# Loading and preparing the first two row groups of a second feed-forward stage together, ahead of its first matmul

## The chip, the cores and the metric

The kernel runs on one core of one Trainium2 chip. The metric is device time in microseconds (us) of one execution; the kernel before has a median of 1038.68 us over 3 runs (1036.22 to 1038.87). In the rows that follow PE is TensorE, DVE is VectorE, ACT is ScalarE, POOL is GpSimd and SP is the engine that issues most DMAs.

## What is computed

Attention of 4 batches, 12 heads, 448 positions and 64 dimensions (causal), then a feed-forward layer in which each of the 1792 tokens goes through one of 8 experts, then a dense feed-forward layer:

```
logits = x @ w_gate;  e_idx = argmax(logits)
out[mask] = gate_w * eom * (relu(x[mask] @ w1[e]) @ w2[e])     # x: 1792 x 768, w1: 768 x 1024
h = x @ w_in                                                    # w_in: 768 x 2048
g = h - tanh(h)
y = g @ w_out                                                   # w_out: 2048 x 768
```

## The kernel before

Products are made of three matmuls of two half-precision parts (hi x hi, lo x hi, hi x lo). A weight or a row is therefore kept as two planes, hi and lo.

**Experts.** `slot` (L816 on) takes one block of 128 tokens through one expert: gathered rows, first product in two halves of four column blocks (`slot_mm1`), each followed by `slot_relu` (hi part `hh` on ScalarE L169, lo part `hl` on VectorE L170), transposes of the next block's rows (`rows_T`), the second product in two halves (`slot_mm2`, 8 blocks of three matmuls of 384 columns), each copied to `yo` by ScalarE (L832), and a store of the rows to `ys_d` in DRAM (L859). The rows of `ys_d` are sorted by expert. Expert e has a static slot and then extra slots under nested conditions (`extra`), as many as its token count asks for; the last expert (e = 7) has one extra slot in this run. Work that belongs to other parts is put between these pieces by `fill(z)`: z = 1 after the second `slot_relu`, 2 and 3 after the two output halves, 4 after the store. The argument `late` turns this on.

**w_in and w_out.** They come as pairs of 32-bit words of a double. `conv` turns 1024 of these into planes: `to_f32` (six VectorE operations on halves, L897, L900, L903), a scaling (`scaled`, ScalarE L113) and the lo part (`rest_of`, VectorE or GpSimd). `conv_load` brings a unit into one of two buffers `cu`, `conv_store` writes its planes (`co`) to `wb_d` in DRAM. The extra slots of expert 6 convert three units each, the static slot of expert 7 the last two that go through DRAM, and two more (`stg`) are converted after the last slot, in place. `wi_load(c)` brings chunk c of w_in (four chunks, 3072 elements in each of `wif[0]` and `wif[1]`, which lie in the experts' raw weight buffers `raw1` and `raw2`) back from `wb_d`; `wo_load(c)` does so for w_out.

**The last stage.** Its 14 row blocks go in groups of 3, 3, 3, 3 and 2. A block is prepared by `prep0` (load from `ys_d`, on SP's queue), `prep1` (maximum of each row and factors from it, VectorE), `prep_hi` (ScalarE), `prep_lo` (VectorE, or GpSimd for group 0), `prep_sc` (exponents, and two 128 x 128 diagonals per block), `prep2` (12 transposes on TensorE and two evictions into `yh` and `yl`) and `prep3` (product of ones with the diagonals, evicted into `rs`). `first_prep` does the first four steps for group 0, in the static slot of expert 7 (`fill(3)`). Group 1's rows are loaded after that slot. Its `prep1` to `prep_sc` run inside steps 0 to 7 of group 0, its `prep2` in steps 9 to 11 and its `prep3` in steps 12 and 13.

The loop over n (16 steps for each group, L1289 on) makes one column block of h per step (`a_mm`, 18 matmuls) and runs the tanh and its correction over four engines (`act_a` to `act_d`, the first operation being VectorE's L1229). From n = 17 on the blocks of w_out's product for the group before (`mm2_step`, L1272) are put between. PE, ACT, DVE and POOL each work strictly in the order in which the program lists their instructions, and SP issues its DMAs in its order too, waiting at each for what it needs.

Of the kernel before, what the change touches and what calls it, by code (L numbers as in the profile page):

```python
# [46 lines left out]
NDY = 22  # L47
# [10 lines left out]
def build(ctx: ExitStack, tc: tile.TileContext, kq0, kq, v, wg, wo, w1, w2, wf, out):  # L58
# [757 lines left out]
    def slot(e, i, w, tag, fill=None, trans=(), then=(), late=False):  # L816
# [21 lines left out]
        lo(0)  # L838
        slot_relu(1, slot_mm1(e, i, 1, w, tag), hh, hl)
# [68 lines left out]

    def conv(src, hi, lo, eng="v"):
        hs = [slice(0, 512), slice(512, 1024)]  # L910
        to_f32([(cc[:, h], src[:, h, :]) for h in hs])
        for h in hs:
            scaled("a", hi[:, h], cc[:, h].bitcast(F32))
        for h in hs:
            rest_of(eng, lo[:, h], cc[:, h].bitcast(F32), hi[:, h])
# [7 lines left out]
    def conv_fill(e, i):  # L923
        c = CPE[e] if e + 1 < E else 0
        n0 = c * (i - 1 - FB[e])
        p = (i - 1) % 2 if c == 3 else 0

        def fill(z):
            for j in range(c):
                if z == ((1,), (1, 3), (1, 2, 3))[c - 1][j]:  # L930
                    b = (p + j) % 2
                    conv(cu[b], co[b][:, 0], co[b][:, 1], "p" if j == 2 else "v")
                    conv_load(cu[b], unit_of(e, n0 + j + min(c, 2)))
                    conv_store(b, unit_of(e, n0 + j))

        return fill
# [28 lines left out]
    yg_of = lambda g, i: first["yg"][i] if g < 2 else yg1  # L965
# [49 lines left out]
    def prep_sc(g, i, n=1):  # L1015
# [5 lines left out]
                                       op0=ALU.mult, op1=ALU.mult)  # L1021
        for j in range(n):
# [4 lines left out]

    def prep2(g, i, tag="t"):
        d = G[g % 2]
        tsl = slice(i * 128, (i + 1) * 128)  # L1030
        planes_T(yq_of(g, i), d["yh"][:, :, tsl], d["yl"][:, :, tsl], tpool[0], tag, "v" if g == 1 else "a")
# [26 lines left out]
    def first_again():  # L1058
        for g in range(2):
            for i in range(GB[g]):  # L1060
                prep0(g, i, (GS[g] + i) * 128)
            if g == 0:
                first_prep()

# [20 lines left out]
    for e in range(E):  # L1085
# [25 lines left out]
        else:  # L1111
# [3 lines left out]
            stg += [wof[1][:, z * 2048 : (z + 1) * 2048] for z in range(2)]  # L1115
            tot = nc.values_load(flg[0:1, 1:2], min_val=0, max_val=NDY)
            remaining()
            first["yg"] = [wof[1][:, z * 2 * DM : (z + 1) * 2 * DM].bitcast(F32) for z in range(3)]
            at_ = (wof[1][:, 6 * DM :], wof[0])
            first["yq"] = [[t[:, z * 2 * DM : (z + 1) * 2 * DM].rearrange("p (k x n) -> p k x n", k=KD, x=2)  # L1120
                            for z in range(3)] for t in at_]
            first["dg"] = [[t[:, 6 * DM + 256 * z : 6 * DM + 256 * (z + 1)].bitcast(BF16).rearrange(
                "p (a n) -> p a n", a=2) for z in range(3)] for t in at_]
            first["sc"] = [t[:, 6 * DM + 768 : 6 * DM + 832].bitcast(F32) for t in at_]
            second = nc.values_load(flg[0:1, 0:1], engines=(SP,), min_val=0, max_val=128)
# [52 lines left out]
    qc = (cc, wof[0][:, 8192:10240].bitcast(U32))  # L1178
# [203 lines left out]
```

## Time and profile before

| | |
|---|---|
| median of 3 runs | 1038.68 us |
| the profiled execution | 1039.69 us |
| its span | 1038.0 us |
| TensorE busy | 985.1 us (95%) |
| VectorE busy | 787.2 us (76%) |
| ScalarE busy | 597.1 us (58%) |
| GpSimd busy | 470.4 us (45%) |
| mean granted TensorE clock | 0.992 |

Times in rows count from the start of the span. A row of the timeline gives start, duration, engine, line, operation, output and inputs, shape and count; what stands in brackets is the idle time of the engine before it and what ended that. A granted clock of 1.00 is full speed. A matmul's duration overlaps that of the next.

### The profile page before, as it was taken

What the parts mean: (1) busy time and instruction counts of PE and PEld (TensorE: products, weight loads), DVE (VectorE), ACT (ScalarE), POOL (GpSimd) and SP (SyncE); (2) the same over time, 40 slices, a digit from 0 to 9 for tenths busy, and PEclk for the clock granted to TensorE, in tenths of its full rate; (3) what the DMA queues carried; (4) which work ended last, traced back from release to release, by engine and by line L of the source; (5) the groups of instructions that cost most, each with busy time, mean ns of one, the idle gap of its engine ahead of it and who ended that gap; (6) DMA issues with size and microseconds to landing.
All of it is one profiled execution on the core that took longest, in us unless ns stands there. A gap on an engine that the chain in (4) does not pass through costs nothing. (4 is left out here: it accounts for less than half of the span.)

```text
span 1038.0 us, 24100 instructions
## 1 busy us (share of the span) xinstructions
PE 985.1 (95%) x9177; PEld 743.5 (72%) x9177; DVE 787.2 (76%) x1609; ACT 597.1 (58%) x1194; POOL 470.4 (45%) x499
## 2 busy tenths in 40 slices
PE   5999999998998999999988889999999999999996
PEld 4999999997777878777866555666666666667763
DVE  6668777786796678778778899887888798776640
ACT  5776777765456266563323679555656566555530
POOL 5475866584211021202228789545544443443321
PEclk9999999999999999999999999999999999999998
DMA  8889998955898879977887514010000000000000
GB/s 250 224 214 255 270 244 229 265 167 144 284 356 318 342 274 332 349 287 248 314 294 277 212 63 158 24 47 16 24 31 32 9 31 9 16 16 17 16 24 23
DMA packets 62646, 173.92 MB, mean 168 GB/s; under 512 B 8368, under 2 KB 23344, under 8 KB 59424
## 3 DMA queue, kind: packets, MB, share of 16 engines
q1 hardware_dynamic: 56352, 147.20, 42.4%
q0 software_dynamic: 6144, 24.84, 8.4%
q8 instruction: 79, 1.29, 0.5%
q14 instruction: 71, 0.58, 0.2%
HBM read 132.30 MB, written 29.62 MB: 156 GB/s over the span
## 5 line engine op out<-in xcount | busy, mean ns | idle before, releaser
L1272 PE MATMUL fo<-wo,g 128*128 128x384 f16 x1344 | 228.2, 326 | 0.0
L1221 PEld LDWEIGHTS <-raw 128*128 128x128 f16 x1440 | 140.7, 98 | 88.5 <-issue 10.1
L1272 PEld LDWEIGHTS <-g 128*128 128x128 f16 x1344 | 131.2, 98 | 83.8
L1231 POOL TENSOR_TENSOR V<-cu,cc 128x384 f32<-128x384 f32 (+1 forms) x80 | 78.7, 984 | 189.3 <-ACT cu L1230 188.5
L162 PEld LDWEIGHTS <-w 128*128 128x128 f16 x2592 | 148.7, 99 | 16.5 <-issue 15.5
L1221 PE MATMUL fh<-cu,raw 128*128 128x384 f16 (+1 forms) x864 | 131.9, 308 | 6.3 <-DVE cc L1229 6.3
L344 ACT ACTIVATE P<-s,nb 112x112 f32<-112x112 f32 (+1 forms) x192 | 89.8, 494 | 54.2 <-DVE nb L338 24.0
L381 PE MATMUL o<-v,PT 112*112 112x65 f32 x960 | 114.6, 259 | 0.0
L381 PEld LDWEIGHTS o<-v,PT 112*112 112x112 f32 x960 | 105.4, 178 | 0.1
L121 DVE SCALAR_TENSOR_TENSOR w<-raw,w 128x768 f16<-128x768 f32 (+1 forms) x99 | 99.0, 1062 | 3.6 <-ACT w L113 3.6
L800 POOL DMA_INDIRECT xg<-xs_d,idx x22 | 27.5, 1250 | 159.9 <-PEq L872 28.6
L1230 ACT ACTIVATE cu<-cc 128x384 f32<-128x384 f32 (+1 forms) x80 | 40.1, 502 | 103.4 <-DVE cc L1229 103.4
L1234 POOL TENSOR_TENSOR X<-cc,X 128x384 f32<-128x384 f32 (+1 forms) x80 | 91.2, 1140 | 4.1 <-ACT X L1233 0.5
L113 ACT ACTIVATE w<-raw 128x768 f16<-128x768 f32 (+2 forms) x106 | 89.1, 904 | 6.3 <-DVE w L121 3.7
L1229 DVE TENSOR_TENSOR cc<-fh,co 128x384 f32<-128x384 f32 (+1 forms) x80 | 42.0, 525 | 66.5 <-PE fh L1221 50.7
L331 DVE TENSOR_REDUCE s<-s 112x2 f32<-112x224 f32 (+1 forms) x144 | 78.9, 548 | 15.0 <-PE s L327 13.8
L1241 DVE SCALAR_TENSOR_TENSOR V<-cu,V 128x384 f32<-128x384 f32 (+1 forms) x80 | 85.2, 1065 | 0.1
L1249 DVE TENSOR_TENSOR V<-V,co 128x384 f32<-128x384 f32 (+1 forms) x64 | 78.3, 1224 | 0.0
L1221 PE MATMUL fh<-yh,raw 128*128 128x384 f16 x384 | 67.6, 326 | 0.7 <-DVE cc L1229 0.7
L362 PE MATMUL t<-ident,P 112*112 112x112 f32 x480 | 66.9, 262 | 0.0
L1250 ACT ACTIVATE g<-V 128x384 f16<-128x384 f32 (+1 forms) x80 | 40.1, 501 | 45.9 <-DVE V L1249 45.8
L325 PE MATMUL s<-kh,qa 128*112 128x112 f16 (+1 forms) x192 | 54.9, 294 | 10.1 <-POOL qa L276 7.0
(657 smaller groups left out, 2038.9 us busy)
## 6 DMA issues: line engine op xcount, KB each, us to landing
raw<-w SPq DMA_DIRECT2D x48, 512.0 KB, 6.8
raw<-w SPq DMA_DIRECT2D x60, 384.0 KB, 9.1
cu<-wf SPq DMA_DIRECT2D x22, 1024.0 KB, 7.1
wb_d<-co SPq DMA_DIRECT2D x22, 512.0 KB, 5.1
raw<-kq SPq DMA_DIRECT2D x11, 896.0 KB, 10.1
raw<-wb_d SPq DMA_DIRECT2D x8, 768.0 KB, 6.5
xs_d<-xq SPq DMA_DIRECT2D x24, 224.0 KB, 5.9
raw<-v SPq DMA_DIRECT2D x11, 448.0 KB, 10.7
```

Of the source, the lines that this page charges most:

```text
L113: nc.scalar.activation(out=out, in_=in_, func=AF.Copy, scale=WS)
L121: nc.vector.scalar_tensor_tensor(out=out, in0=in_, scalar=WS, in1=hi, op0=ALU.mult, op1=ALU.subtract)
L162: nc.tensor.matmul(out=ph[:, (f % 4) * 128 : (f % 4 + 1) * 128], lhsT=w[0][:, ww, k, f * 128 : (f + 1) * 128], rhs=xTs[tag][:, xx, k, :], ...
L331: nc.vector.tensor_reduce(out=d["nm", m], in_=d["s", m], op=ALU.max, axis=AX.X, negate=True)
L344: nc.scalar.activation(out=d["P"][:, j, OFF[i] : OFF[i] + n], in_=d["s", m][:, z, :], func=AF.Exp, bias=d["nb"][:, 2 * i + j : 2 * i + j + ...
L381: nc.tensor.matmul(out=po[:, i, :], lhsT=d["PT"][:, g, o : o + CP], rhs=d["t"][3][:, hl, j, :], start=(j == 0), stop=(j == i))
L1221: nc.tensor.matmul(out=ph[:, 0:nt], lhsT=wi[ww][:, f // 4, k, f % 4 * 128 : (f % 4 + 1) * 128], rhs=yy[:, k, 0:nt], start=(q == 0), stop=( ...
L1231: nc.gpsimd.tensor_tensor(out=d["V"], in0=d["U"], in1=d["h"], op=ALU.mult)
L1234: nc.gpsimd.tensor_tensor(out=d["X"], in0=d["h"], in1=d["X"], op=ALU.subtract)
L1241: nc.vector.scalar_tensor_tensor(out=d["V"], in0=d[f"S{z}"], scalar=QD[z - 1], in1=d["V"], op0=ALU.add, op1=ALU.mult)
L1249: nc.vector.tensor_tensor(out=d["V"], in0=d["V"], in1=rs_y(g, nt), op=ALU.mult)
L1272: nc.tensor.matmul(out=po[:, 0:384], lhsT=t[:, x, k, i * 128 : (i + 1) * 128], rhs=wo_[ww][:, k, z * 384 : (z + 1) * 384], start=(k == 0 a ...
```

## The change

Group 0's and group 1's rows now lie in w_in's chunks 2 and 3 (`rows_`), their planes in w_out's second buffer and in chunk 2 of `wif[1]`. All six loads go out at the start of the last expert. In its static slot a conversion is put between the two halves of the first product (new `fill(0)`, with a second buffer for the converted words), `first_prep` moves from `fill(3)` to `fill(2)`, and group 1's `prep1` goes into `fill(3)`. Chunks 0 and 1 of w_in are loaded after that slot, chunk 3 at step 0 and chunk 2 at step 4. After the last slot come group 0's diagonals on ScalarE (`prep_dg`), group 1's hi planes, the two staged conversions (scaled by ScalarE, VectorE before), group 1's exponents and lo planes, and only then group 0's transposes; then the lo parts of the staged units and group 1's diagonals. Group 1's transposes are in steps 2 to 4 (hi plane evicted by ScalarE, VectorE before) and its `prep3` in steps 5 and 6. In the extra slots of expert 6 the third unit's load and store move behind the store of the rows.

```diff
@@ slot
         hi(1)
         lo(0)
+        fill(0)
         slot_relu(1, slot_mm1(e, i, 1, w, tag), hh, hl)
@@ conv_fill
-                if z == ((1,), (1, 3), (1, 2, 3))[c - 1][j]:
-                    b = (p + j) % 2
+                at = ((1,), (1, 3), (1, 2, 3))[c - 1][j]
+                b = (p + j) % 2
+                if z == at:
                     conv(cu[b], co[b][:, 0], co[b][:, 1], "p" if j == 2 else "v")
+                if z == (4 if at == 3 else at):
                     conv_load(cu[b], unit_of(e, n0 + j + min(c, 2)))
                     conv_store(b, unit_of(e, n0 + j))
@@ prep_sc
+        if n > 1:
+            nc.vector.tensor_scalar(out=c(7), in0=c(2), scalar1=1.0 / WS, scalar2=None, op0=ALU.mult)
+            return
...
+    def prep_dg(g, i, n):
+        b0, s, c = prep_s(g, i, n)
+        for j in range(n):
+            dg = dg_of(g, i + j)
+            for x, z in ((0, 7), (1, 5)):
+                nc.scalar.activation(out=dg[:, x, :], in_=identh, func=AF.Copy, scale=s[:, z, j : j + 1])
@@ prep2
-        planes_T(yq_of(g, i), d["yh"][:, :, tsl], d["yl"][:, :, tsl], tpool[0], tag, "v" if g == 1 else "a")
+        planes_T(yq_of(g, i), d["yh"][:, :, tsl], d["yl"][:, :, tsl], tpool[0], tag)
@@ the last expert
+            rows_ = [wif[z][:, o : o + row] for z, o in
+                     ((0, 9216), (0, 9216 + row), (1, 9216), (1, 9216 + row), (0, 6144), (0, 6144 + row))]
...
+            for g in range(2):
+                for i in range(GB[g]):
+                    prep0(g, i, second * (GS[g] + i) if g + i else 0)
             tot = nc.values_load(flg[0:1, 1:2], min_val=0, max_val=NDY)
             remaining()
...
-            for i in range(GB[0]):
-                prep0(0, i, second * i if i else 0)
+            qc = (cc, wof[0][:, 8192:10240].bitcast(U32))
 
             def fill(z):
-                if z == 2:
+                if z < 2:
+                    to_f32([(qc[z][:, h], cu[z][:, h, :]) for h in HS])
+                if z in (1, 2):
+                    conv_planes(qc[z - 1], co[z - 1][:, 0], co[z - 1][:, 1], "p")
+                    conv_store(z - 1, nc.values_load(flg[0:1, z + 1 : z + 2], engines=(SP,), min_val=0, max_val=NDY - 1))
+                if z == 1:
                     for q in range(2):
                         conv_load(stg[q], NDY + q, nc.gpsimd)
-                if z in (1, 2):
-                    conv(cu[z - 1], co[z - 1][:, 0], co[z - 1][:, 1], "p")
-                    conv_store(z - 1, nc.values_load(flg[0:1, z + 1 : z + 2], engines=(SP,), min_val=0, max_val=NDY - 1))
+                if z == 2:
+                    first_prep()
                 if z == 3:
-                    first_prep()
+                    prep1(1, 0, GB[1], False)
@@ after the static slot of the last expert
-            wi_load(nc.sync, 0)
-            for i in range(GB[1]):
-                prep0(1, i, second * (GB[0] + i))
+            for c in range(2):
+                wi_load(nc.sync, c)
         extra(e, 1 + FB[e], wts[e])
+    prep_dg(0, 0, GB[0])
+    for j in range(GB[1]):
+        prep_hi(1, 0, GB[1], j)
     for q in range(2):
         to_f32([(qc[q], stg[q])])
-        scaled("v", qhl[q][0], qc[q].bitcast(F32))
-        if q:
-            for prep in (prep2, prep3):
-                for i in range(GB[0]):
-                    tpool[0] = (mp_t, mp_y, mp_h)[i]
-                    prep(0, i, "tys"[i])
+        scaled("a", qhl[q][0], qc[q].bitcast(F32))
+    prep_sc(1, 0, GB[1])
+    for j in range(GB[1]):
+        prep_lo(1, 0, GB[1], j)
+    for prep in (prep2, prep3):
+        for i in range(GB[0]):
+            tpool[0] = (mp_t, mp_y, mp_h)[i]
+            prep(0, i, "tys"[i])
+    for q in range(2):
         rest_of("p", qhl[q][1], qc[q].bitcast(F32), qhl[q][0])
+    prep_dg(1, 0, GB[1])
@@ the loop over n
-            if n in (9, 10, 11):
-                prep2(1, (9, 10, 11).index(n))
-            for i in {12: (0, 1), 13: (2,)}.get(n, ()):
+            if n in (2, 3, 4):
+                prep2(1, n - 2)
+            for i in {5: (0, 1), 6: (2,)}.get(n, ()):
                 prep3(1, i)
...
-        if n == 0:
-            prep1(1, 0, GB[1], False)
-        if n in (1, 3, 5):
-            prep_hi(1, 0, GB[1], (1, 3, 5).index(n))
...
-        if n in (3, 5, 7):
-            prep_lo(1, 0, GB[1], (3, 5, 7).index(n))
-        if n == 2:
-            prep_sc(1, 0, GB[1])
-        if g == 0 and f < 3:
-            wi_load(nc.sync, f + 1)
+        if n in (0, 4):
+            wi_load(nc.sync, {0: 3, 4: 2}[n])
```

Three places show what this does to the order on the engines. The first is SP's queue at the end of an extra slot of expert 6, the fourth, which is the last that runs here (`cu_4955` and `cu_4956` are the two buffers `cu`, `co_4958` and `co_4959` the two buffers `co`). Before:

```order
L918 DMA wb_d<-co_4958 256x1x1024
L921 TENSOR_LOAD xtab
L921 ISA x2
L907 ISA
L907 DMA cu_4956<-wf 128x2048
L921 TENSOR_LOAD xtab
L921 ISA x2
L918 ISA
L918 DMA wb_d<-co_4959 256x1x1024
L858 ISA
L859 DMA ys_d<-yo_I-17077_17078 128x768
```

and now:

```order
L923 DMA wb_d<-co_4958 256x1x1024
L859 ISA
L860 DMA ys_d<-yo_I-17077_17078 128x768
L926 TENSOR_LOAD xtab
L926 ISA x2
L908 ISA
L908 DMA cu_4956<-wf 128x2048
L926 TENSOR_LOAD xtab
L926 ISA x2
L923 ISA
L923 DMA wb_d<-co_4959 256x1x1024
```

The store of the rows has moved ahead of the load into the second buffer `cu` and of the last store of planes. The second place is VectorE in the static slot of expert 7, from its first lo half on. Before:

```order
L170 SCALAR_TENSOR_TENSOR hl_I-17754_17755<-ph_I-17758_17759,hh_I-17752_17753 128x512
L170 SCALAR_TENSOR_TENSOR hl_I-17754_17755<-ph_I-17834_17835,hh_I-17752_17753 128x512
L151 COPY xT_4482<-pt_I-17919_17920 128x768
L897 TENSOR_SCALAR cc<-cu_4955 128x512 x2
L900 SCALAR_TENSOR_TENSOR cc<-cu_4955,cc 128x512 x2
L903 SCALAR_TENSOR_TENSOR cc<-cu_4955,cc 128x512 x2
L897 TENSOR_SCALAR cc<-cu_4956 128x512 x2
```

and now:

```order
L170 SCALAR_TENSOR_TENSOR hl_I-17757_17758<-ph_I-17761_17762,hh_I-17755_17756 128x512
L898 TENSOR_SCALAR cc<-cu_4955 128x512 x2
L901 SCALAR_TENSOR_TENSOR cc<-cu_4955,cc 128x512 x2
L904 SCALAR_TENSOR_TENSOR cc<-cu_4955,cc 128x512 x2
L170 SCALAR_TENSOR_TENSOR hl_I-17757_17758<-ph_I-17843_17844,hh_I-17755_17756 128x512
L151 COPY xT_4482<-pt_I-17928_17929 128x768
L898 TENSOR_SCALAR wo_17683<-cu_4956 128x512 x2
L901 SCALAR_TENSOR_TENSOR wo_17683<-cu_4956,wo_17683 128x512 x2
L904 SCALAR_TENSOR_TENSOR wo_17683<-cu_4956,wo_17683 128x512 x2
L990 TENSOR_REDUCE wo_17684<-raw_89 128x1 x2
```

The first conversion has moved between the two lo halves, and the second writes another buffer. The third place is ScalarE after the last slot, up to the evictions of group 0's diagonal products (`raw_89` and `raw_90` hold `wif[0]` and `wif[1]`, `wo_17683` and `wo_17684` w_out's buffers). Before:

```order
L153 ACTIVATE cu_4955<-pt_I-19412_19413 128x6x128
L153 ACTIVATE cu_4955<-pt_I-19430_19431 128x6x128
L153 ACTIVATE cu_4955<-pt_I-19448_19449 128x6x128
L1038 ACTIVATE co_4958<-rsp_I-19466_19467 128x2x128
L1038 ACTIVATE co_4958<-rsp_I-19470_19471 128x2x128
L1038 ACTIVATE co_4958<-rsp_I-19474_19475 128x2x128
```

and now:

```order
L1043 ACTIVATE wo_17684<-identh,wo_17684 128x128 x6
L1004 ACTIVATE raw_90<-raw_90,wo_17684 128x6x128
L1004 ACTIVATE raw_90<-raw_89,wo_17684 128x6x128
L1004 ACTIVATE wo_17684<-raw_89,wo_17684 128x6x128
L113 ACTIVATE wo_17683<-cc 128x1024
L113 ACTIVATE wo_17683<-wo_17683 128x1024
L153 ACTIVATE cu_4955<-pt_I-19433_19434 128x6x128
L153 ACTIVATE cu_4955<-pt_I-19451_19452 128x6x128
L153 ACTIVATE cu_4955<-pt_I-19469_19470 128x6x128
L1055 ACTIVATE co_4958<-rsp_I-19487_19488 128x2x128
L1055 ACTIVATE co_4958<-rsp_I-19491_19492 128x2x128
```

Six diagonals, group 1's three hi planes and the two scalings have come in ahead of group 0's evictions.

## Rows read from the trace of the kernel before

**Rows 1.** The chain of waits in time order: start us, duration us, what.

```profile
600.76 1.21 DVE wo L1005
...
635.56 3.09 PE fh L1221 x18
```

**Rows 2.** Timeline, group 0: VectorE's L1229 of steps 0, 3, 9, 10, 14, 15.

```profile
576.37 0.56 DVE L1229 TENSOR_TENSOR cc<-fh,co 128x384 f32<-128x384 f32 x1 [3.00 <-POOL scm L115]
...
590.02 0.55 DVE L1229 TENSOR_TENSOR cc<-fh,co 128x384 f32<-128x384 f32 x1
...
613.58 0.54 DVE L1229 TENSOR_TENSOR cc<-fh,co 128x384 f32<-128x384 f32 x1
...
617.56 0.54 DVE L1229 TENSOR_TENSOR cc<-fh,co 128x384 f32<-128x384 f32 x1
...
631.54 0.54 DVE L1229 TENSOR_TENSOR cc<-fh,co 128x384 f32<-128x384 f32 x1
...
634.97 0.54 DVE L1229 TENSOR_TENSOR cc<-fh,co 128x384 f32<-128x384 f32 x1
```

**Rows 3.** Timeline, TensorE: the first product of steps 0 to 2.

```profile
573.15 8.94 PE L1221 MATMUL fh<-cu,raw 128*128 128x384 f16 x54
```

**Rows 4.** Timeline of the last expert's extra slot: VectorE, ScalarE, TensorE.

```profile
551.53 2.66 DVE L983 TENSOR_REDUCE wo<-wo 128x1 f32<-128x768 f32 x3
...
556.18 2.59 ACT L997 ACTIVATE wo<-wo 128x768 f16<-128x768 f32 x3 [3.48 <-issue]
...
559.30 0.50 PE L174 MATMUL py_I-18271_18272<-w,hh_I-18095_18096 128*128 128x384 f16 x2 [1.93 <-ACT hh_I-18095_18096 L169]
...
560.03 0.34 PE L174 MATMUL py_I-18271_18272<-w,hl_I-18097_18098 128*128 128x384 f16 x1 [0.23 <-DVE hl_I-18097_18098 L170]
```

**Rows 5.** Timeline of the last expert's static slot: TensorE and VectorE.

```profile
540.71 0.49 PE L174 MATMUL py_I-17951_17952<-w,hh_I-17752_17753 128*128 128x384 f16 x2
...
540.87 0.69 DVE L170 SCALAR_TENSOR_TENSOR hl_I-17754_17755<-ph_I-17834_17835,hh_I-17752_17753 128x512 f16<-128x512 f32 x1 [3.27 <-ACT hh_I-17752_17753 L169]
...
541.94 0.75 DVE L897 TENSOR_SCALAR cc<-cu 128x512 uint32<-128x512 uint32 x2
...
543.81 1.29 DVE L903 SCALAR_TENSOR_TENSOR cc<-cu,cc 128x512 uint32<-128x512 uint32 x2
```

**Rows 6.** Timeline after the extra slot: ScalarE and TensorE.

```profile
567.72 0.49 ACT L832 ACTIVATE yo_I-18099_18100<-py_I-18298_18299 128x384 f32<-128x384 f32 x1 [3.41 <-PE py_I-18298_18299 L174]
...
570.27 0.51 PE L149 MATMUL pt_I-19421_19422<-identh,wo 128*128 128x128 f16 x6 [1.46 <-POOLq L872]
...
571.86 0.80 ACT L153 ACTIVATE cu<-pt_I-19448_19449 128x768 f16<-128x768 f16 x1
```

**Rows 7.** SP's timeline; landing times of the 22 loads of line L907.

```profile
529.38 0.35 SPq L907 DMA_DIRECT2D cu<-wf  x1
...
538.77 0.46 SPq L859 DMA_DIRECT2D ys_d<-yo_I-17077_17078  x1
...
545.14 1.56 SPq L972 DMA_DIRECT2D wo<-ys_d  x3
...
DMA to landing us min/median/max: 5.1/7.1/11.5
```

**Rows 8.** ScalarE's groups by shape (busy us, mean ns); its timeline.

```profile
L113 ACT ACTIVATE w<-raw 128x1024 f16<-128x1024 f32 x42 | 42.0, 1054 | 2.3 <-ACTq L872 2.0 <-PE ph_I-15727_15728 L162 0.3
...
572.55 0.39 ACT L1038 ACTIVATE co<-rsp_I-19466_19467 128x256 bf16<-128x256 f32 x1
...
573.08 0.41 ACT L1038 ACTIVATE co<-rsp_I-19474_19475 128x256 bf16<-128x256 f32 x1
```

**Rows 9.** TensorE by windows: length, busy (instructions), clock, DMA share, GB/s.

```profile
530.00:530.50 0.50, 0.00 (x0) 1.00 1.27 369
...
531.00:531.50 0.50, 0.40 (x4) 0.50 0.88 315
...
534.00:534.50 0.50, 0.50 (x9) 0.73 0.92 352
```

More of the change, by code (lines that the diff above doesn't have):

```diff
@@ L907, in conv_load, with conv_planes @@
         eng.dma_start(out=dst.rearrange("p n t -> p (n t)").unsqueeze(1), in_=wf32[:, ds(r, 1), :])
-    def conv(src, hi, lo, eng="v"):
[L910 to L915, printed above, removed]
+    HS = [slice(0, 512), slice(512, 1024)]
+    def conv_planes(c, hi, lo, eng):
+        for h in HS:
+            scaled("a", hi[:, h], c[:, h].bitcast(F32))
+        for h in HS:
+            rest_of(eng, lo[:, h], c[:, h].bitcast(F32), hi[:, h])
+    def conv(src, hi, lo, eng="v"):
+        to_f32([(cc[:, h], src[:, h, :]) for h in HS])
+        conv_planes(cc, hi, lo, eng)
     def conv_store(b, r):
@@ L963, in wo_load @@
                           in_=wb_d[:, z, NI + c * 3 : NI + q1, :])
-    yg_of = lambda g, i: first["yg"][i] if g < 2 else yg1
+    yg_of = lambda g, i: first["yg"][g][i] if g < 2 else yg1
     yq_of = lambda g, i: first["yq"][g][i] if g < 2 else G["yq"]
@@ L1063, in first_again @@
                 first_prep()
+            else:
+                prep1(1, 0, GB[1], False)
     def order_b():
@@ L1115, in build @@
             stg += [wof[1][:, z * 2048 : (z + 1) * 2048] for z in range(2)]
+            row = 2 * DM
+            rows_ = [wif[z][:, o : o + row] for z, o in
+                     ((0, 9216), (0, 9216 + row), (1, 9216), (1, 9216 + row), (0, 6144), (0, 6144 + row))]
+            first["yg"] = [[t.bitcast(F32) for t in rows_[3 * g : 3 * g + 3]] for g in range(2)]
+            planes_ = [[wof[1][:, 2048 + z * row : 2048 + (z + 1) * row] for z in range(3)],
+                       [wif[1][:, 6144 : 6144 + row], wif[1][:, 6144 + row : 6144 + 2 * row], wof[1][:, 6656 : 6656 + row]]]
@@ new lines, in build @@
+            first["yq"] = [[t.rearrange("p (k x n) -> p k x n", k=KD, x=2) for t in ts] for ts in planes_]
+            first["dg"] = [[wof[1][:, 8192 + 768 * g + 256 * z : 8448 + 768 * g + 256 * z].bitcast(BF16).rearrange(
+                "p (a n) -> p a n", a=2) for z in range(3)] for g in range(2)]
+            first["sc"] = [wof[1][:, 9728 + 64 * g : 9792 + 64 * g].bitcast(F32) for g in range(2)]
+            second = nc.values_load(flg[0:1, 0:1], engines=(SP,), min_val=0, max_val=128)
+            for g in range(2):
+                for i in range(GB[g]):
+                    prep0(g, i, second * (GS[g] + i) if g + i else 0)
@@ L1116, in build @@
             tot = nc.values_load(flg[0:1, 1:2], min_val=0, max_val=NDY)
             remaining()
[L1118 to L1123, printed above, removed]
@@ L1124, in build @@
-            first["sc"] = [t[:, 6 * DM + 768 : 6 * DM + 832].bitcast(F32) for t in at_]
-            second = nc.values_load(flg[0:1, 0:1], engines=(SP,), min_val=0, max_val=128)
-            for i in range(GB[0]):
-                prep0(0, i, second * i if i else 0)
-            def fill(z):
-                if z == 2:
+            qc = (cc, wof[0][:, 8192:10240].bitcast(U32))
+            def fill(z):
+                if z < 2:
[4 more added lines that the diff above has]
+                if z == 1:
@@ L1131, in fill @@
                     for q in range(2):
                         conv_load(stg[q], NDY + q, nc.gpsimd)
-                if z in (1, 2):
-                    conv(cu[z - 1], co[z - 1][:, 0], co[z - 1][:, 1], "p")
-                    conv_store(z - 1, nc.values_load(flg[0:1, z + 1 : z + 2], engines=(SP,), min_val=0, max_val=NDY - 1))
+                if z == 2:
+                    first_prep()
                 if z == 3:
-                    first_prep()
+                    prep1(1, 0, GB[1], False)
```

1 line of the change is left out of this document (removed).

## Prediction

> **What bounds the kernel now.** I read the chain of waits first, then the timeline around the place where the chain changes its character, then the DMA issues and the granted clock there. From 635.56 to the end the chain runs on TensorE alone, blocks of the first and of the second product in turn [rows 1]; whatever the change gains or loses has to be gained or lost before that point, and from there on it is handed through to the end unchanged, since no work of groups 1 to 4 is taken off TensorE. Before it, in the first group of the last stage (group 0), the chain runs through VectorE, ScalarE and GpSimd, and group 1's preparing stands in it [rows 1]. The pace there is best read from VectorE's line L1229, the first operation of every step: step 0 is at 576.37 and step 15 at 634.97, so 15 steps take 58.6. The last step alone takes 3.43 (631.54 to 634.97), the first three together 13.65 (576.37 to 590.02), and one with a row block's transposes and evictions 3.98 (613.58 to 617.56) [rows 2]. TensorE is not the limit in these steps: 54 matmuls take 8.94, which is 2.98 for the 18 of a step and 0.166 for one [rows 3].
>
> Two stalls ahead of it matter. In the expert's extra slot TensorE waits 1.93 for ScalarE, which is busy with three high planes of group 0 (2.59 from 556.18), and 0.23 more for VectorE [rows 4]. After that slot TensorE waits 1.46 for the last GpSimd low plane, and its first matmul of the last stage is at 573.15, 5.4 after ScalarE's last output of the slot (567.72) [rows 3, 6].
>
> The sum is made against the profiled execution, 1039.69, whose span is 1038.0 with 1.69 around it; the median of the runs is 1038.68, 1.01 lower, so the sum's difference is taken from the median at the end. About 0.3%, or 3.1, is what a measurement of this kernel can tell from no change.
>
> **The change, part by part.** Differences are in us, minus is faster.
>
> A. Conversion between the two halves of the static slot of the last expert. VectorE stands idle for 3.27 ahead of its second low half (540.87), that is from 537.60 [rows 5]. The six operations put there take 3.16 (541.94 to 545.10) [rows 5], so they end at 540.76 and fit. Their input must have landed by then: the order of SP's queue shows that the buffer needed is the one loaded by the last load but one, issued at 529.38; with the median of 7.1 it lands at 536.5, with the slowest, 11.5, at 540.9 [rows 7]. In that case the second half's low part is ready at 540.9 + 3.16 + 0.69 = 544.7. TensorE, which starts its second layer at 540.71, needs it after four blocks of three matmuls and two more, 14 times 0.166 = 2.3 later, at 543.0 [rows 3, 5]. So I take 0; the ends are 0 and +1.7.
>
> B. The extra slot. Group 0's factors and planes are now asked for after the first output column of the static slot, with VectorE's conversions out of the way. VectorE's work ahead of the extra slot's first low half is then: the second conversion from 541.94 to 545.10, group 0's factors (4.65, from the first reduction at 551.53 to ScalarE's first plane at 556.18), a little for the exponents, group 1's factors (again 4.65) [rows 4, 5]: 545.1 + 9.3 + 0.5 = 554.9. TensorE's mm1 and transposes end at 559.30 - 1.93 = 557.37 [rows 4]. Even if GpSimd stretches VectorE by 1.5 the low half is there in time, and ScalarE's planes (2.59) lie at about 550 to 553, ahead of the relu. The whole 2.16 can go; I take -2.0, with ends -2.16 and -0.5 (VectorE 2 late). The row loads for this: the store that they wait for is issued at 538.77 now [rows 7]. It is moved past a load and a store that wait for VectorE and GpSimd, so it goes some 5 earlier, and so do the row loads, now at 545.14, while twice as many are issued (3 for the six); with the 7.1 of the larger loads [rows 7] group 1's rows are there at about 550, when they are wanted. What is hidden there is looked at again under the rivals.
>
> C. Between the extra slot and the first matmul. This is where the change adds. On ScalarE, which works in order, six diagonals, group 1's three high planes and two scalings of 1024 now stand between the slot's last output and the three evictions that the first matmul needs. The row's price of a high plane is 2.59 / 3 = 0.86 [rows 4], of a 1024 scaling 1.05, and three 256-wide activations start 0.265 apart (572.55 to 573.08, two steps) [rows 8]. A 128-wide one lies between half of that and all of it; I take 0.2. So: last output 0.49, diagonals 6 x 0.2 = 1.2, planes 2.6, scalings 2.1, evictions 3 x 0.8 = 2.4 [rows 6], and 0.5 from the end of the last eviction (572.66) to the matmul (573.15) [rows 3, 6]: 9.3 in place of 5.4, **+3.9**. With the ends of the diagonals (0.8 and 1.6) and evictions that overlap a little it is +3.2 to +4.4. The wait of 1.46 for GpSimd goes, since GpSimd starts its low planes some 5 earlier, but it is inside the 5.4 and is not counted again. VectorE has in the same time two more conversions of the kind that took 3.16, three low planes (0.69 for 512 elements [rows 5], so 1.04 for 768) and three evictions: 11 to 12 from about 559, against a first matmul at about 575. That covers it with some 4 to spare; if GpSimd stretches it by half, nothing is left.
>
> [...] No row here shows a 128-wide activation out of SBUF.
>
> D. The clock. TensorE now stands nearly idle from the end of its transposes, at about 568, to 573.5. Where it last stood idle so (busy 0.00 in the half microsecond from 530.0), its granted clock was then 0.50 (1.2 of 2.4 GHz) from 531.0, and 0.73 in the half microsecond from 534.0, so 3.25 at half speed [rows 9]. Here the work that follows is dense, so half of that is lost: **+1.6**. The ends are 0 (the clock does not fall, as in the stretch with the wait of 1.46, which is shorter) and +1.6.
>
> E. The steps of group 0. Group 1's factors, planes, low planes and diagonals leave them; its transposes move from steps 9 to 11 to steps 2 to 4, with the high plane evicted by ScalarE and no longer by VectorE. The new 15 steps: the first is TensorE's 2.98; the second has a matmul block and two sets of six transposes on TensorE (0.51 for one set alone [rows 6], less when they follow each other) and an eviction, 4.2; two more with transposes at 3.98 each; eleven at 3.43. That is 2.98 + 4.2 + 7.96 + 37.7 = 52.9 against 58.6: **-5.7**. At best all steps take 3.43 (51.4, -7.2). At worst three of them take 1.1 more, since ScalarE's 0.80 and VectorE's part do not overlap, and the first is no shorter (54.7, -3.9).
>
> The w_in chunks: two are now loaded ahead of the extra slot, the fourth at step 0, the third at step 4. The third is wanted at step 8, four steps or 13.7 later, and a load of this kind of size takes at most 11.5 [rows 2, 7], so it costs nothing. w_out's loads only come free earlier. The moved store and load of experts' last fill change no order that TensorE waits for.
>
> Sum: 0 - 2.0 + 3.9 + 1.6 - 5.7 = **-2.2**. Profiled execution 1037.5; against the median 1038.68 - 2.2 = **1036.5**. With all best ends -6.2 (1032.5), with all worst ones +3.3 (1042.0).
>
> **The rivals.**
>
> R1, clearly faster. The clock stays full, because the transposes and diagonal products lie spread in the gap, and the steps with transposes hardly exceed 3.43, ScalarE having some room in a step. Then D is 0 and E about -6.7: -4.8, 1033.9. For it: after the gap with 1.46 of waiting the matmuls ran at full pace, 0.166 each [rows 3, 6]. Against it: this gap is three times as long.
>
> R2, slower: rows that land late. The reductions of both groups now stand on VectorE ahead of the extra slot's low halves, so a late row holds TensorE. The store may fail to move forward, or the six loads queue behind it: if they go out at 545.14 as now, take 3 to issue and then the slowest landing of the table, 11.5 [rows 7], group 1's rows are there at 560, its factors at 564.3, the low half at 565, 7.3 after TensorE wants it: 0 + 7.3 - 2.16 + 3.9 + 1.6 - 5.7 = +4.9, 1043.6. It is slower by over 0.3% from a landing at about 558 on. Against it: the usual landing is half of that, and the store's place in the queue is plainly earlier.
>
> R3, even: ScalarE paces the steps. Each step already gives it six operations, three steps gain 0.80 each, and the gap in front is its own work. Then E is -3.9 and the sum -0.4, 1038.3. This is also where the time ends if the preparing was hidden anyway.
>
> **How the numbers follow.** The forecast has 0.46, R1 0.32, R3 0.12, R2 0.10. Of the forecast's own spread (1034.5 to 1038.5) a small part, 0.05, lies beyond -3.1, and so does R1: faster 0.37. Slower is R2 and the far end of the worst case, 0.11. Within 0.3% is the rest, 0.52. The range takes in the forecast, R1 and R3 with their bounds and leaves most of R2 out: 1032.0 to 1040.5.
>
> **What would show it.** Right: no wait of TensorE for ScalarE in the extra slot; its end about 2 earlier; the first matmul of the last stage about 2 later than 573.15, after ScalarE's evictions; granted clock 0.50 for about 3 there; L1229 of step 15 about 2 earlier than 634.97, and equal spacing of 3.43 from step 5 on. Wrong: a first matmul at or before 573 (C too high), full clock (R1), VectorE idle before its reductions with a load as releaser (R2), or steps of 4 and more (R3).

## The result, and the profile after

The changed kernel takes 1047.95 us (median of 19 runs, 1043.42 to 1055.43), the kernel before 1041.25 (19 runs, 1036.22 to 1048.84); the ratio is **1.006, 95% interval 1.0039 to 1.0082**: slower by 0.6%, where 1036.5 had been forecast, with a range of 1032.0 to 1040.5. Both kernels spread more than the first three runs showed. The profiled executions are 1044.14 (span 1042.4, clock 0.986) and 1039.69 (span 1038.0).

Step 15 of group 0 still decides the end: it starts at 639.41 instead of 634.97, 4.44 later, and the span is 4.4 longer. The timeline of the changed kernel, VectorE's first operation (now L1262) of steps 0, 10 and 15, answers to [rows 2]:

```profile
587.83 0.56 DVE L1262 TENSOR_TENSOR cc<-fh,co 128x384 f32<-128x384 f32 x1 [6.45 <-PE fh L1254]
...
622.29 0.55 DVE L1262 TENSOR_TENSOR cc<-fh,co 128x384 f32<-128x384 f32 x1
...
639.41 0.55 DVE L1262 TENSOR_TENSOR cc<-fh,co 128x384 f32<-128x384 f32 x1
```

The steps gained what was promised: 51.6 from step 0 to step 15 instead of 58.6. But step 0 is 11.5 later than before. ScalarE's timeline after the extra slot, which answers to [rows 6], shows where:

```profile
567.13 0.49 ACT L832 ACTIVATE yo_I-18104_18105<-py_I-18303_18304 128x384 f32<-128x384 f32 x1 [3.41 <-PE py_I-18303_18304 L174]
567.89 1.86 ACT L1043 ACTIVATE wo<-identh,wo 128x128 bf16<-128x128 f16 x6 [0.27 <-ACTq L873]
576.14 1.76 ACT L1004 ACTIVATE raw<-raw,wo 128x768 f16<-128x768 f32 x2 [6.39 <-issue]
...
578.63 1.04 ACT L113 ACTIVATE wo<-cc 128x1024 f16<-128x1024 f32 x1
...
580.52 0.79 ACT L153 ACTIVATE cu<-pt_I-19433_19434 128x768 f16<-128x768 f16 x1
```

Between the diagonals (L1043) and group 1's high planes (L1004) ScalarE waits 6.39, and the row names no cause ("issue"). The rest of the way from the last output to the first matmul is nearly as long as forecast, 9.7 for 9.3. TensorE, same stretch, answers to [rows 3]; ahead of it the two rows that answer to [rows 4]:

```profile
555.22 0.50 PE L174 MATMUL py_I-18276_18277<-w,hh_I-18100_18101 128*128 128x384 f16 x2 [0.38 <-ACT hh_I-18100_18101 L169]
557.76 0.34 PE L174 MATMUL py_I-18276_18277<-w,hl_I-18102_18103 128*128 128x384 f16 x1 [2.05 <-DVE hl_I-18102_18103 L170]
...
581.36 0.37 PE L1054 MATMUL rsp_I-19487_19488<-wo,onesb 128*128 128x256 bf16 x1 [11.46 <-ACT cu L153]
...
583.24 10.30 PE L1254 MATMUL fh<-cu,raw 128*128 128x384 f16 x54
```

The first matmul is at 583.24, 16.1 behind ScalarE's last output of the slot (5.4 before). In the extra slot the wait for ScalarE has nearly gone (0.38 for 1.93), but one of 2.05 for VectorE has taken its place, and behind it the granted clock falls to 0.50 (windows in the last section). VectorE's timeline from the second conversion to the first low half:

```profile
541.55 1.75 DVE L898 TENSOR_SCALAR wo<-cu 128x512 uint32<-128x512 uint32 x2 [1.55 <-DMA cu<-wf]
...
545.63 1.91 DVE L990 TENSOR_REDUCE wo<-raw 128x1 f32<-128x768 f32 x2
547.96 0.95 DVE L990 TENSOR_REDUCE wo<-raw 128x1 f32<-128x768 f32 x1 [0.42 <-DMA raw<-ys_d]
...
552.36 2.66 DVE L990 TENSOR_REDUCE wo<-raw 128x1 f32<-128x768 f32 x3
...
557.03 0.68 DVE L170 SCALAR_TENSOR_TENSOR hl_I-18102_18103<-ph_I-18106_18107,hh_I-18100_18101 128x512 f16<-128x512 f32 x1
```

**What else ends at 576.** SyncE's timeline in the changed kernel, the loads of w_in's chunks 0 and 1:

```profile
562.99 2.12 SPq L963 DMA_DIRECT2D raw<-wb_d  x4
```

what SyncE does where the skipped extra slots end, line 873 (operations of that line, 555 to 600 us: shortest, median and longest in ns, first and last start in us):

```profile
L873 SPq EVENT_SEMAPHORE  x8: 17/17/17, 570.5 to 576.3; - x8
```

and the transfers, by windows of the same kernel (length, busy and count by engine, clock, DMA share, GB/s):

```profile
572.00:573.00 1.00, 0.00 (x0) 0.00 (x0) 0.00 (x0) 0.00 (x0) 0.00 (x0) 0.67 0.97 372
573.00:574.00 1.00, 0.00 (x0) 0.00 (x0) 0.00 (x0) 0.00 (x0) 0.00 (x0) 0.50 0.42 169
574.00:575.00 1.00, 0.00 (x0) 0.00 (x0) 0.00 (x0) 0.00 (x0) 0.00 (x0) 0.50 0.07 28
575.00:576.00 1.00, 0.00 (x0) 0.00 (x0) 0.00 (x0) 0.00 (x0) 0.00 (x0) 0.50 0.04 15
576.00:577.00 1.00, 0.00 (x0) 0.00 (x0) 0.00 (x0) 0.86 (x2) 0.00 (x0) 0.50 0.00 0
```

The last packet lands just before 576, SyncE's last event there is at 576.3, and ScalarE goes on at 576.14. The list of instructions with their waits says how these hang together (SyncE's first, then ScalarE's first high plane of group 1; DMAHW0 to 7 are the semaphores of SyncE's transfers):

```
L873 UNCONDITIONAL_BRANCH [waits DMAHW0_49,DMAHW1_49,DMAHW2_49,DMAHW3_49,DMAHW4_49,DMAHW5_49,DMAHW7_49]
L1004 ACTIVATE raw2_90<-raw2_90,wo_1_17684 128x6x128 [waits DMAHW7_49,DMAHW3_49,DVE_49]
```

Group 1's rows can come from two loads: the one at the start of the last expert, and the one that `first_again` issues behind extra slots that this run skips. The plane waits for a semaphore of each. On the skipped path SyncE raises the second itself. It goes through its semaphores in turn and waits at each for the transfers under way on it, w_in's chunks among them. (The branch listed is the innermost one. The one that this run takes has DMAHW6 as well: eight, as many as the events in the trace.) This waiting is called the join below.

The semaphore that the plane lacks is DMAHW3, the fourth in turn. By the single events in the trace SyncE passed the first four at 570.49, 572.40, 575.10 and 576.05, and ScalarE went on at 576.14. The transfer on the fourth is not a load of w_in: it is the extra slot's own store of rows (L860, issued at 567.64), which went out behind those loads and landed after them. So the last 0.95 of the wait is that store's.

### The profile page after: what moved, and what is told of

Its sections match the earlier page's. It is cut to its first block, busy times and chain, and to the rows that moved or that the text cites. A ratio compares the mean times of both kernels' runs of the same rounds, so it can differ in the third digit from the quotient of the medians.

```text
span 1042.4 us, 24107 instructions
## 1 busy us (share of the span) xinstructions
PE 985.8 (95%) x9177; PEld 744.6 (71%) x9177; DVE 782.6 (75%) x1594; ACT 604.1 (58%) x1211; POOL 467.3 (45%) x499
## 3 DMA queue, kind: packets, MB, share of 16 engines
q0 software_dynamic: 6144, 24.84, 8.3%
## 5 line engine op out<-in xcount | busy, mean ns | idle before, releaser
L1262 DVE TENSOR_TENSOR cc<-fh,co 128x384 f32<-128x384 f32 (+1 forms) x80 | 42.1, 526 | 72.2 <-PE fh L1254 59.5
```

## The experiments

Three theories were set against each other. **T1**: the 6.39 are this join. **T2**: they are ScalarE's own branches and instruction fetch. **T3**: ScalarE waits for the rows themselves or for VectorE. T2 was the author's supposition; no run had shown it.

In the table, times count from ScalarE's last output of the slot ahead of the last expert's static slot (the anchor, us in the profile), because what lies ahead of it differs by up to 14 us from run to run. "End" is ScalarE's last output of the extra slot, steps are VectorE's first operation. These times are of the one profiled execution of each kernel, the ratio is of all its runs (95% interval), and the two do not always go together: e1_one_early stands at +109.39 with a ratio of 0.9999, e11_planes_dg at +102.57 with 0.9994.

| kernel | anchor | end | first matmul | step 0 | step 15 | ratio to before |
|---|---|---|---|---|---|---|
| before | 529.69 | +38.03 | +43.46 | +46.68 | +105.28 | 1 |
| changed | 528.10 | +39.03 | +55.14 | +59.73 | +111.31 | 1.0060 (1.0039 to 1.0082) |
| e1_one_early | 531.26 | +42.05 | +52.10 | +57.80 | +109.39 | 0.9999 (0.9971 to 1.0028) |
| e2_twice | 529.09 | +36.23 | +61.38 | +67.06 | +118.62 | one run |
| e3_first_ahead | 527.56 | +37.60 | +42.79 | +53.13 | +109.08 | 1.0010 (0.9984 to 1.0036) |
| e4_both | 541.94 | +37.88 | +43.06 | +53.53 | +105.57 | 1.0004 (0.9968 to 1.0040) |
| e5_order | 533.13 | +36.76 | +41.95 | +46.71 | +102.66 | 0.9968 (0.9942 to 0.9994) |
| e6_late_max | 529.73 | +36.49 | +41.67 | +48.92 | +106.19 | 1.0009 (0.9976 to 1.0041) |
| e7_diag_back | 535.61 | +36.07 | +40.76 | +47.32 | +104.66 | 0.9999 (0.9980 to 1.0019) |
| e8_diag_vector | 529.05 | +38.39 | +53.33 | +57.96 | +109.57 | one run |
| e9_late_max2 | 540.19 | +35.48 | +40.70 | +47.93 | +102.47 | 0.9951 (0.9922 to 0.9979) |
| e10_planes_late | 533.48 | +37.09 | +42.28 | +45.50 | +103.30 | 0.9959 (0.9917 to 1.0001) |
| e11_planes_dg | 527.83 | +39.04 | +42.88 | +46.10 | +102.57 | 0.9994 (0.9960 to 1.0028) |
| e12_combined | 532.43 | +36.12 | +40.81 | +47.38 | +101.17 | 0.9937 (0.9918 to 0.9956) |

**e1_one_early: half the bytes.**

```diff
-            for c in range(2):
-                wi_load(nc.sync, c)
+            wi_load(nc.sync, 0)
         extra(e, 1 + FB[e], wts[e])
+    wi_load(nc.sync, 1)
```

> Only chunk 0 of w_in is loaded ahead of the extra slot; chunk 1's two loads are issued behind it, ahead of the preparing block. Theory T1 (SyncE, which passes the skipped levels of extra slots, waits there until every transfer it has under way has landed, and ScalarE's high planes of group 1 wait for a semaphore that SyncE raises only after that): half the bytes are under way, so they land some 4 us after their issue instead of 12.5; ScalarE's first high plane of group 1 starts at 570 to 571 instead of 576.14 (idle 0.3 to 1 instead of 6.39), the first matmul of the last stage at 577 to 578 instead of 583.24, and the span is 5 to 6 shorter: 1036 to 1037. Rival T2 (the 6.39 us are ScalarE's own branches and instruction fetch): start at 576 as before, span 1042. Rival T3 (the high planes wait for group 1's rows themselves or for VectorE): 576 as well.

**e2_twice: the same loads twice.** `for c in (0, 1, 0, 1): wi_load(nc.sync, c)`.

> Chunks 0 and 1 of w_in are loaded twice ahead of the extra slot (the same bytes to the same place; nothing of the result changes). T1: the high planes of group 1 start only when the second set has landed, 8 to 11 us later than 576.14, so at 584 to 587, and the span is 8 to 11 longer than 1042.4: 1050 to 1053. T2 and T3: the high planes start at 576 as before; since the first matmul itself then waits for the second set, the span may be longer by 1 to 4 but not ScalarE's wait.

ScalarE's first high plane of group 1 in the timeline of e1_one_early, and of e2_twice:

```profile
576.26 1.76 ACT L1004 ACTIVATE raw<-raw,wo 128x768 f16<-128x768 f32 x2 [0.33 <-issue]
```

```profile
583.36 1.76 ACT L1004 ACTIVATE raw<-raw,wo 128x768 f16<-128x768 f32 x2 [15.41 <-SPq L873]
```

SyncE's line 873 in e2_twice:

```profile
L873 SPq EVENT_SEMAPHORE  x8: 17/17/17, 575.3 to 583.3; - x8
```

With half the bytes the wait is 0.33, with twice the transfers 15.41; there the profile names SyncE's line 873, whose last event at 583.3 is where ScalarE goes on (584 to 587 was expected). ScalarE's branches and group 1's row loads are the same in all three, and VectorE had stood idle since 567.8 in e2_twice, so T2 and T3 fall with that run. ScalarE's own branches took little: the idle time that its line 873 ended, ahead of the diagonals, is 0.27 in all three.

e1_one_early would not have decided it alone. Its plane started at 576.26 and its first matmul at 583.36, where T2 and T3 had them, and not at 570 to 571 and 577 to 578; the span was 1043.7 for 1036 to 1037. The reason is that its extra slot ended at +42.05: the rows landed late there (VectorE stood 1.87 and 1.31 for them), and TensorE waited 2.91 and 1.81. The way from the slot's end to the first matmul is 10.05, 6.06 shorter than in the changed kernel. About half of that is an earlier join (the plane at +45.0 instead of +48.0 from the anchor), the other half the later end of the slot. What SyncE stood for last was the slot's own store (issued at 573.82, passed at 576.17). Over 12 runs the ratio is 0.9999, 0.6% below that of the changed kernel, and the intervals do not overlap.

**e3_first_ahead and e4_both: group 0's transposes, evictions and `prep3` written ahead of group 1's planes**, with both chunks early (e3) or one (e4).

> Group 0's transposes, their evictions and its scale rows are written ahead of group 1's high and low planes; both chunks are loaded early as in the changed kernel. T1: the evictions of group 0 need no semaphore that is raised behind the joins, so ScalarE's first eviction starts at 570 to 570.5, and the first matmul waits for the landing of the chunks alone, at 575.5 to 576.5 instead of 583.24; the high planes still start at about 576. Span 6 to 7.5 shorter than 1042.4: 1035 to 1036.5. T2: the idle 6.4 us stand ahead of the first eviction instead, first matmul at 578.5 to 579.5, span 1038 to 1039.

> Both edits: chunk 1 loaded behind the extra slot, and group 0's transposes and evictions ahead of group 1's planes. T1: first eviction at 570 to 570.5, first matmul at 572.5 to 573.5 (573.15 in the kernel before), the fifteen steps in 51.6 to 53, the span 9.5 to 11 shorter than 1042.4: 1031.5 to 1033, faster than the kernel before by 5 to 6.5. T2: first matmul at 578.5 to 579.5, span 1038 to 1039.

The evictions did not wait for the join, so the first matmul came at +42.8 and +43.1, much as in the kernel before (+43.5), and in e3 5 ahead of what was expected (570.35 for 575.5 to 576.5). But step 0 came 10.3 and 10.5 behind it, where the kernel before has 3.2 and the changed one 4.6. Neither ratio differs from 1, so the gains expected, 5 to 6.5 on the kernel before for e4, did not come. The cause is the edit: it also put VectorE's two conversions (8 us, under the extra slot until then) behind the evictions, with the low planes behind both. In e3 the low planes still waited for the join as well.

**e5_order: conversions and small products ahead again, then group 0, then group 1's planes, scalings and low planes**, chunk 1 late as in e1.

> As e1_one_early (chunk 1 loaded behind the extra slot), and VectorE's conversions of the last two w_out units and group 1's small products stay ahead, then group 0's transposes, evictions and scale rows, then group 1's high planes, the two scalings, the low planes. Times are counted from ScalarE's last output of the slot ahead of the last expert's static slot (529.69 in the kernel before, where step 15 follows at +105.3; 528.10 and +111.3 in the changed one; e4_both, whose conversions stood behind the evictions, had +105.6), since what lies ahead of it differs from run to run by several us. T1 (only SyncE's join and the order behind it were lost): extra slot's end at +37.5 to +42, first matmul 5 to 6 behind it, step 0 on VectorE 3.2 to 5 behind that, 51.6 to 53 from there to step 15: +98 to +104, ratio to the kernel before 0.993 to 0.999. Rival T4 (what is moved behind the first matmul comes back in the steps, because ScalarE has 4.6 us of planes and scalings in front of step 0): 56 to 58 from step 0 to step 15, step 15 at +103 to +107, ratio 0.999 to 1.002.

Faster than the kernel before: 0.9968, in T1's range, with an interval that just leaves out 1. Step 0 came 4.8 behind the first matmul, as T1 had it; the 15 steps took 55.95, which is T4's side. VectorE's and GpSimd's timeline in e5_order:

```profile
588.13 1.33 DVE L1275 SCALAR_TENSOR_TENSOR V<-S,V 128x384 f32<-128x384 f32 x1 [5.89 <-POOL V L1265]
...
579.76 1.18 POOL L129 TENSOR_TENSOR wo<-scm,wo 128x512 f16<-128x512 f32 x1 [8.89 <-ACT wo L113]
```

GpSimd's low halves of the last w_out units stand ahead of the first product of step 0 there and wait for ScalarE's scalings, which stand behind the planes. Under the join's wait this had been hidden.

**e6_late_max and e7_diag_back: group 1's reductions behind the extra slot**; in e7 group 0's diagonals on VectorE too.

```diff
-                if z == 3:
-                    prep1(1, 0, GB[1], False)
```

> As e5_order, but group 1's reductions leave the static slot and stand on VectorE behind group 0's evictions; its high planes follow step 0, its low planes step 1, its diagonals step 2, its transposes steps 3 to 7. Theory B1 (the 4.7 us of group 1's reductions stand on VectorE ahead of the extra slot's low halves, and TensorE waits for those): the extra slot ends at +35.5 to +37 every time, with a wait for VectorE below 0.4 and none of TensorE's clock lost there; first matmul 5 to 6 behind. Steps 52 to 55 if T1 holds, so step 15 at +96.5 to +101, ratio 0.990 to 0.996. Rival B2 (the extra slot waits for ScalarE or for the rows' landing whatever stands on VectorE): end at +38 to +40, step 15 at +100 to +104. T4: steps 56 to 58.6 as in the kernel before, step 15 at +101 to +104.

> As e6_late_max, with group 0's six diagonals made on VectorE in the static slot as in the kernel before. If the diagonals on ScalarE stand on the path (1.86 for six between the extra slot's last output and the first eviction), the first matmul comes 3.5 to 4.2 behind the extra slot's end instead of 5 to 6, and step 15 and the span are 1.2 to 1.9 shorter than e6_late_max; VectorE's 1.5 to 2.3 more in the static slot cost at most 1. If they cost nothing there (TensorE's transposes or GpSimd's join end last), the two are alike within 0.5.

B1 holds: ends at +36.5 and +36.1, in e7 with no wait of TensorE in the second product. The steps missed (57.3 in both): VectorE's first low plane of e6_late_max shows why.

```profile
586.89 1.02 DVE L1012 SCALAR_TENSOR_TENSOR raw<-raw,wo 128x768 f16<-128x768 f32 x1 [7.24 <-DMA raw<-wb_d]
```

Chunk 3's load stands ahead of these planes in both kernels, and their rows lie under it, so that a block's low plane is made there from chunk 3's bytes: the two are of use for their times alone. e9 loads chunk 3 later. The diagonals on ScalarE cost 0.5 behind the slot (5.18 for 4.69), not 1.2 to 1.9: TensorE's transposes run beside them (566.81 to 569.82 in e6_late_max, the diagonals 566.98 to 568.84).

**e8_diag_vector: the changed kernel with its diagonals undone.**

> The changed kernel with this one part undone: group 0's diagonals on VectorE again, in the static slot. T1: the high planes of group 1 wait for SyncE's join, which waits for the two chunks, and these are issued behind GpSimd's conversions; so neither ScalarE's 1.86 less nor VectorE's 1.5 to 2.3 more moves anything: high planes at +47 to +50, first matmul 7 to 7.3 behind them, step 15 at +110.5 to +113 as in the changed kernel (+48.0, +55.1, +111.3). Rival (the chain of ScalarE alone sets the first matmul, diagonals included): first matmul 1.9 earlier, step 15 at +109.4; or, with VectorE's longer queue ahead of the extra slot's low halves, 2 later.

```profile
575.28 1.76 ACT L1004 ACTIVATE raw<-raw,wo 128x768 f16<-128x768 f32 x2 [7.34 <-SPq L873]
...
562.28 2.43 SPq L963 DMA_DIRECT2D raw<-wb_d  x4
```

ScalarE's wait (timeline, with SyncE's row of the chunks) grew to 7.34 and is put down to line 873. The first matmul is 7.1 behind the planes as in the changed kernel. It came 1.8 earlier from the anchor, just outside what T1 expected, and the chunks went out 1.7 earlier from it too (+33.2 for +34.9), so it follows them. By its times alone this run does not exclude the rival, whose +109.4 it meets; the row does, since ScalarE stood idle for 7.34 right ahead of the planes.

**e9_late_max2: chunk 3 after step 1, chunk 2 after step 5.**

> As e6_late_max, with chunk 3 of w_in loaded at the end of step 1 and chunk 2 at the end of step 5, so that group 1's low planes no longer stand behind chunk 3's landing (VectorE waited 7.24 for it in e6_late_max, and made one block's low plane there from bytes that chunk 3 had already replaced). B1: the extra slot ends at +36 to +36.7 from the anchor (ScalarE's last output of the slot ahead of the static one), as in e6_late_max (+36.5) and e7_diag_back (+36.1). Step 0 at +48 to +49.5, since group 1's reductions stand on VectorE ahead of it; 52 to 54.5 from step 0 to step 15 if the wait for chunk 3 was what the steps lost there (57.3 in e6_late_max): step 15 at +100.5 to +103.5, ratio to the kernel before 0.994 to 0.999. Rival T4 (preparing group 1 among the first steps costs what it cost in the kernel before, whatever the order): 56 to 58.6, step 15 at +104.5 or more, ratio 0.999 to 1.003.

**e10_planes_late: reductions in the static slot again, scalings directly behind group 0's evictions, group 1's planes among the steps; e11_planes_dg: with group 0's diagonals on VectorE.**

> As e5_order (step 15 at +102.7 from the anchor; there GpSimd's four low halves of the last two w_out units waited for ScalarE's scalings behind the high planes, and the first product of step 0 on GpSimd came 17.2 behind the extra slot's end, VectorE waiting 5.89 for it): now the two scalings follow group 0's evictions directly, and group 1's high planes follow step 0, its low planes step 1, its diagonals step 2, transposes in steps 3 to 7, chunks 3 and 2 loaded after steps 1 and 5. Theory P (GpSimd's 7.8 us of low halves decide when the steps begin to flow): first product on GpSimd 13 to 14.5 behind the extra slot's end, step 0 to step 15 in 51.6 to 53.5, step 15 at 61 to 63 behind the extra slot's end (65.9 in e5_order): +98 to +101.5, ratio 0.992 to 0.996. Rival T4: what is put among the steps costs there what it saved, 55 to 57, ratio 0.996 to 1.000.

> As e10_planes_late, with group 0's six diagonals on VectorE in the static slot as in the kernel before. In e7_diag_back the first matmul came 4.7 behind the extra slot's end instead of 5.2: 0.5 is saved behind the slot. VectorE's queue ahead of the extra slot's low halves is 1.5 to 2.3 longer, and with group 1's reductions in it TensorE waits for it (2.05 in the changed kernel, 2.42 in e8_diag_vector): the extra slot's end 0 to 2.3 later than in e10_planes_late. Net between 0.5 faster and 2 slower than e10_planes_late. If the slot's end does not move, VectorE's queue is not what holds it, but the rows' landing.

e9 came out close to what was expected (end +35.5 for +36 to +36.7, step 0 +47.9 for +48 to +49.5, 54.5 for the steps, step 15 and ratio inside) and is faster than the kernel before by 0.5%. e10 speaks against P, though its ratio lies in P's range: GpSimd's first product came 15.4 behind the end (585.96), not 13 to 14.5, and the steps took 57.8, T4's side. In e11 the end went back to +39.0 with TensorE waiting 2.45 for VectorE.

**e12_combined: e9 and e7's diagonals.**

> As e9_late_max2, with group 0's six diagonals on VectorE in the static slot. Where group 1's reductions stand in the static slot, the diagonals there pushed the extra slot's end out (e11_planes_dg: +39.0 from the anchor, TensorE waiting 2.45 for VectorE); where they do not (e7_diag_back) it stayed at +36.1. So here: extra slot's end at +35.5 to +36.5, first matmul 4.5 to 4.8 behind it (5.2 in e9_late_max2), 61 to 62 from the first matmul to step 15 as in e5_order, e9_late_max2 and e10_planes_late (60.7, 61.8, 61.0), step 15 at +101.3 to +103, ratio to the kernel before 0.993 to 0.998: the same as e9_late_max2 within what can be measured. If the diagonals on VectorE hold the low halves here too, the end is at +37.5 to +39 and the ratio 0.997 to 1.000.

TensorE's only wait in the second product of the extra slot in e12_combined:

```profile
560.86 0.34 PE L174 MATMUL py_I-18271_18272<-w,hl_I-18097_18098 128*128 128x384 f16 x1 [0.20 <-DVE hl_I-18097_18098 L170]
```

0.9937 (0.9918 to 0.9956; 6 runs against 11): faster than the kernel before by 0.6%, and its interval lies wholly below that of the changed kernel. Against e9 nothing more is shown; the intervals overlap.

## Why the prediction was wrong

In the profiles, from the anchor, the change costs +6.0 at step 15 (+111.31 for +105.28), which is the 0.6% measured; the forecast was -2.2. The base of the forecast was low as well: the kernel before has a median of 1041.25 over 19 runs, 2.6 above the 1038.68 of three, so 2.6 of the 11.4 between 1036.5 and 1047.95 are that base.

- **A** held: the conversion between the halves cost nothing.
- **B** was -2.0 and came out at +1.0. The step "545.1 + 9.3 + 0.5 = 554.9" failed in both parts: the second conversion waited 1.55 for its load, and the two sets of factors took 11.4 (545.63 to 557.03), while TensorE wanted the low half at 555.7. So TensorE's two waits in the slot are 2.43 together, not gone from 2.16. Behind them the fallen clock cost 1.7, which the sum had in D alone: from the low half's first matmul to the slot's last output it is 9.37 (557.76 to 567.13), before 7.69. The slot's first product ended 0.95 earlier from the anchor; 0.3 + 1.7 - 0.95 is the +1.0. The path is R2's, VectorE's reductions ahead of the low halves, but not R2's cause: a late row held VectorE for 0.42 only. That group 1's reductions make the difference the experiments show: with them in the static slot (nine kernels) TensorE waits 0.31 to 2.45 for the low half and the extra slot ends at +36.2 to +42.1; the longest of these waits, 2.42 and 2.45, are in e8 and e11, where VectorE makes the diagonals as well. Without them (e6, e7, e9, e12) TensorE waits 0.23 at most for it and the slot ends at +35.5 to +36.5.
- **C** is the step that failed: +3.9 forecast, +10.7 measured. "On ScalarE, which works in order" followed the engine's own work and asked for no wait. Of the 16.1 the join is 6.39. Almost without it (0.33) e1_one_early needs 10.05, where the forecast had 9.3; 0.66 of the rest are the diagonals, 1.86 for six instead of 1.2.
- **D** held: 4.6 from the first matmul to step 0 instead of 3.2, so +1.4 for +1.6.
- **E** held and was a little better: 51.6 for 52.9, 3.43 a step from step 6 on.

Together 0 + 1.0 + 10.7 + 1.4 - 7.0 = +6.1. The trace of before already had the join, and a row that showed it. SyncE's operations of that line (872 in that kernel), and VectorE's timeline:

```profile
L872 SPq EVENT_SEMAPHORE  x8: 17/17/17, 574.8 to 578.3; - x8
```

```profile
577.87 2.67 DVE L983 TENSOR_REDUCE wo<-wo 128x1 f32<-128x768 f32 x3 [0.94 <-SPq L872]
```

The join ends at 578.3, 5 behind the first matmul [rows 3]. Its first reader there was VectorE, whose reductions of group 1 stood between steps 0 and 1 and waited 0.94 for it. The change moved the first reader of these semaphores ahead of the first matmul and put twice as much of w_in in front of them.

E's gain is also less than it looks. In e1_one_early the steps take 7.0 less than before, and the way from the extra slot's end to step 0 takes 7.1 more (15.75 for 8.65). From the extra slot's end to step 15 it is 67.3 before, 67.3 in e1, 65.9 in e5, 67.0 in e9, 66.2 in e10 and 65.1 in e12, whether group 1 is prepared ahead of the first matmul (steps 51.6) or among the steps (54 to 58); e3, e4, e6 and e7, with the faults named above, have 67.7 to 71.5. What left the steps had to be done in front of them. e5, e9 and e12 gain 1.3, 2.6 and 1.9 on the kernel before by an earlier end of the extra slot and 1.4, 0.3 and 2.2 behind it; e11 gains 3.7 behind it and loses 1.0 in the slot. What sets that remaining length, among VectorE, GpSimd and ScalarE, was not taken apart.

## What to carry to other kernels

When a step is moved ahead, list the semaphores it waits on and what raises each: in this kernel the reader of a tile that a skipped branch could have written waits for that branch's end, and the engine that passes it waits for the transfers that it has under way, its own stores included (6.39 in the changed kernel, 15.41 with the loads made twice, 0.33 with half the bytes). Transfers that the next work does not need are best issued behind such a place, and readers of such tiles put behind work that does not cross it. Work taken out of a paced loop is a gain only where something covers it: in e1_one_early 7.0 left the steps and 7.1 came ahead of them.

## What the runs showed of the hardware

- The same wait is put down to "issue" in the changed kernel (6.39) and e3 (6.25), and to SyncE's line 873 in e2 (15.41) and e8 (7.34). An idle time with "issue" can be a semaphore wait.
- Four loads of 768 KB and the store of rows issued behind them kept the DMA engines full until about 573.5 (share 0.94 from 571 to 572, 0.97 from 572 to 573); then thirteen packets ran on one after another until 575.7 (share 0.07 and 0.04), five of 6144 bytes, which is a row of these loads, and after them eight of 3072, which is a row of that store. For whoever waits for all of it the tail is 2 us.
- A wait of TensorE of 2.05, with 0.38 just ahead, cost clock as well in the changed kernel: windows of its extra slot show 0.50 behind it, where matmuls of 384 columns start 0.32 apart (0.16 at 1.00, in e8_diag_vector's extra slot). In e5_order a wait of 1.88 and in e8_diag_vector one of 2.42 at the same place left it at 1.00; what makes the difference is not shown. The windows of the changed kernel:

```profile
557.00:558.00 1.00, 0.24 (x2) 0.18 (x3) 1.00 (x3) 0.00 (x0) 0.82 (x3) 1.00 0.09 33
558.00:559.00 1.00, 1.00 (x7) 0.57 (x6) 0.77 (x2) 0.00 (x0) 0.90 (x2) 0.85 0.01 2
559.00:560.00 1.00, 1.00 (x4) 0.44 (x3) 0.79 (x1) 0.00 (x0) 0.92 (x2) 0.50 0.07 18
...
562.00:563.00 1.00, 1.00 (x7) 0.63 (x6) 1.00 (x1) 0.00 (x0) 0.92 (x2) 0.95 0.37 148
```
